# Chunked attention and a leaky two-layer MLP on one core: the order of the steps behind the first layer laid down anew, and wider filler matmuls

## The chip, the core and the metric

The kernel runs on one core of a Trainium2 chip. The core has a TensorE (PE in the profile), a VectorE (DVE), a ScalarE (ACT), a GpSimd (POOL) and a SyncE (SP), which run side by side and wait for each other by semaphores. The metric is the device time of one execution in microseconds; three runs are given and their median is compared.

## The reference

`q`, `k` and `v` have 8 batches, 8 heads, 576 rows and 64 columns. The rows are cut into chunks of 64, and each chunk attends only to itself. The result, laid out as 4608 tokens of 512 values, goes through two matrix products with a leaky ReLU between them.

```python
scores = scale * np.matmul(q_c, k_c.transpose(0, 1, 2, 4, 3))
scores = scores - np.max(scores, axis=-1, keepdims=True)
attn = np.exp(scores)
attn = attn / (np.sum(attn, axis=-1, keepdims=True) + 1e-09)
out = np.matmul(attn, v_c)
x = np.ascontiguousarray(attn_out.transpose(0, 2, 1, 3)).reshape(B * S, H * D)
h = x @ w_in                      # 4608x512 times 512x2048
g = np.maximum(0.01 * h, h)
return (g @ w_out).astype(np.float32)   # 2048x512
```

## The kernel before

**Groups.** Attention works on 36 groups of 128 tokens (two chunks), numbered u from 0. A group goes through named steps. `arrive u 0` and `arrive u 1` load q and k on the POOL queue (`load_rows`, L93). For groups 0 to 9 PE transposes them (`pe_t`, L406 and L411, into the PSUM tiles `qp` and `kp`) and ACT or DVE copies them out (`p`, L118 and L120, into QZ; `k`, L420, into KT). From group 10 on two DMA transposes on SP do it (`t u 0`, L430, into QT; `t u 1`, L433, into KT), and two POOL copies `p u 0` and `p u 1` (L446) put QT into QZ. Then come the scores `s u` on PE (L453, tile `Sp`), the maximum `m` and the subtraction `b` on DVE (L463, L467), the exponential `x` on ACT (L473), the sum and its reciprocal `z` on DVE (L479 to L483), the scaling `n` on POOL or DVE (L489, tile `en`), a transpose (`e` on PE and `d2`, or a DMA transpose `d` on SP, L508, tile `et`), the product with V `v` on PE (L519, tile `xp`) and the copy `a` on ACT into xT (L532).

**Blocks.** The MLP works on 12 blocks, four of 128 tokens and eight of 512. Blocks 0 to 5 do the first layer plainly (`mm1`, L187, tile `hT`; ACT applies the leaky ReLU, `g`, L198). Blocks 6 to 11 do it by seven half-size products (`f`, L325, tiles `hA`, `hB`, `hC`) with sums of weights (`vf`) and of inputs (`xf`, L285). Blocks 0 to 3 do the second layer plainly (`mm2`, L212, tile `oP`), blocks 4 to 11 by seven products (`m2`, L373, tiles `oA`, `oB`, `oC`) with sums `wf` and `sf`. Finished sides of a block go out by `save` on SP (L385; L391 for the last block, in six pieces).

**Order.** Nothing is decided while the kernel runs: a table `ORDER` lists every step once, with the PSUM bank or buffer that it takes, and the engines carry out their own steps in that order. A second table `ON` names the engine of those steps that could run on several. An entry such as `(86, (21, 0), 0)` puts filler matmuls ahead of step 86: 21 pieces of 128 columns into bank 0. They are made by `idle` (L538) in matmuls of up to 512 columns on constants, and their result is not used. Step 86 is `pe_t 0 1`, the first transpose on PE.

```python
def idle(n, tag):
    t = bank([128, 512], "idle", tag)
    while n:
        w = min(n, 4) * 128
        nc.tensor.matmul(out=t[:, :w], lhsT=ones[:, :128], rhs=ones[:, :w], start=True, stop=True)
        n -= w // 128
```

In the table before there are fillers ahead of `pe_t 0 1` (21 pieces), `s 0` (3), `pe_t 3 0` (47), `s 2` (13), `e 1` (9), `v 0` (9) and `v 1` (6).

Of the kernel before, what the change touches and what calls it, by code (L numbers as in the profile page):

```python
# [16 lines left out]
def kernel(  # L17
# [25 lines left out]
    NQI = 4  # L43
# [5 lines left out]
    SUB = {4: 256, 5: 256, **{j: 256 for j in range(6, 12)}}  # L49
# [3 lines left out]
    FAST = {6: 4, 7: 4, 8: 4, 9: 4, 10: 4, 11: 4}  # L53
    UNIT = {6: 256, 7: 256}
    POOL_N, POOL_X, POOL_S = 9, 20, 20
# [15 lines left out]
    qk: dict[int, tuple[bass.AP, bass.AP]] = {}  # L71

    WIN: dict[int, bass.AP] = {}

    def window(w):

        if w not in WIN:
            WIN[w] = sbp.tile([128, 2 * H * D], FP16, name="q_in", tag="q_in", bufs=NQI)
        return WIN[w]
# [4 lines left out]
    def k_tile():  # L84
        return sbp.tile([128, H, D], FP16, name="k_in", tag="k_in", bufs=NIN)
# [9 lines left out]
    def load_pairs(w):  # L95
        t = window(w).rearrange("p (h e) -> p h e", h=H)
        for a, z, b, r in cuts(2 * w * G, 2 * (w + 1) * G):
            p0, n = (a - 2 * w * G) // 2, (z - a) // 2
            nc.gpsimd.dma_start(out=t[p0:p0 + n], in_=q[b, :, r:r + z - a, :].rearrange("h (p e) d -> p h (e d)", e=2))

    def load_q(u):
        load_rows(q_tile(u), q, u)
        qk[u] = (q_tile(u), qk[u][1] if u in qk else None)

    def load_k(u):
        t = k_tile()
        load_rows(t, k, u)
        qk[u] = (qk[u][0] if u in qk else None, t)
# [49 lines left out]
    qk[0] = (q_tile(0), k_tile())  # L158
# [11 lines left out]
    def gT(j):  # L170
        n = START[j] // 512
        if n not in GT:
            GT[n] = sbp.tile([128, NFC, 512], FP16, name="gT", tag="gT", bufs=2)
        return GT[n][:, :, START[j] % 512:START[j] % 512 + BLOCKS[j]]

    def sub(j):
        return SUB.get(j, BLOCKS[j])
# [42 lines left out]
    def osb_tile():  # L220
        return sbp.tile([128, 2, d_model], FP32, name="osb", tag="osb", bufs=3)
# [58 lines left out]
    def x_form(j, h, i):  # L280
        (x11, x12), (x21, x22) = x_halves(j, h)
        f = x_sums(j, h)

        def less(to, a, b):
            (nc.gpsimd if j >= POOL_X else nc.vector).tensor_tensor(out=to, in0=a, in1=b, op=ALU.subtract)  # L285

        if i == 0:
            less(f[:, 0], x12, x11)
        elif i == 1:
            less(f[:, 1], x22, f[:, 0])  # L290
        elif i == 2:
# [47 lines left out]
    def g_form(j, i):  # L339
# [38 lines left out]
    def osb(j, side):  # L378
        if (j, side) not in OSB:
            OSB[j, side] = osb_tile()  # L380
        return OSB[j, side]
# [21 lines left out]
    def stage_tq(u, tag="qp"):  # L403
        QP[u] = psp.tile([128, 4, 2, CH], FP16, name="qp", tag=tag, bufs=1)
        for i in range(4):
            nc.tensor.transpose(out=QP[u][:, i, :, :], in_=qk[u][0][:, 2 * i:2 * i + 2, :], identity=ident)  # L406

    def stage_tk(u, tag="kp"):
        KP[u] = psp.tile([128, 4, 2, CH], FP16, name="kp", tag=tag, bufs=1)
        for i in range(4):  # L410
            nc.tensor.transpose(out=KP[u][:, i, :, :], in_=qk[u][1][:, 2 * i:2 * i + 2, :], identity=ident)  # L411
# [6 lines left out]
    def stage_k(u):  # L418
        KT[u] = sbp.tile([128, 4, 2, CH], FP16, name="KT", tag="KT", bufs=4)
# [4 lines left out]
    def stage_t(u, i):  # L424
        if i == 0:
            QT[u // 2] = sbp.tile([128, H, 128], FP16, name="QT", tag="QT", bufs=2)
            nc.sync.dma_start_transpose(out=QT[u // 2], in_=WIN.pop(u // 2))
        elif i == 2:
            QT[u] = sbp.tile([128, H // 2, 128], FP16, name="QT", tag="QT", bufs=4)
            nc.sync.dma_start_transpose(out=QT[u], in_=qk[u][0].rearrange("p h d -> p (h d)"))  # L430
        else:
            KT[u] = sbp.tile([128, 4, 2, CH], FP16, name="KT", tag="KT", bufs=4)
            nc.sync.dma_start_transpose(  # L433
                out=KT[u].rearrange("p i e t -> p i (e t)"), in_=qk[u][1].rearrange("p h d -> p (h d)")
            )
# [35 lines left out]
    def stage_x(u):  # L471
        E[u] = sbp.tile([128, 8, CH], FP16, name="ex", tag="ex", bufs=2)
# [4 lines left out]
    def stage_z(u):  # L477
        z = sbp.tile([128, 8], FP32, name="z", tag="z", bufs=2)
        nc.vector.tensor_reduce(out=z, in_=E[u], axis=AXL.X, op=ALU.add)  # L479
        ze = sbp.tile([128, 8], FP32, name="ze", tag="ze", bufs=2)  # L480
        nc.vector.tensor_scalar_add(out=ze, in0=z, scalar1=1e-9)
        ZI[u] = sbp.tile([128, 8], FP32, name="zi", tag="zi", bufs=2)
        nc.vector.reciprocal(out=ZI[u], in_=ze)  # L483

    def stage_n(u, e):
        ex = E.pop(u)
        eng = nc.gpsimd if e == "pool" else nc.vector
        E[u] = sbp.tile([128, 8, CH], FP16, name="en", tag="en", bufs=3)
# [17 lines left out]
    def stage_d(u):  # L506
        et = sbp.tile([128, 2, 2, 2, CH], FP16, name="et", tag="et", bufs=4)
# [33 lines left out]
    def cast_q():  # L541
        nc.vector.tensor_copy(out=qk[0][0], in_=first[0])

    def cast_k(h):
        half = slice(4 * h, 4 * h + 4)
        if h == 0:
            nc.vector.tensor_copy(out=qk[0][1][:, half], in_=first[1][:, half])
        else:
            nc.scalar.activation(out=qk[0][1][:, half], in_=first[1][:, half], func=AFT.Copy, bias=0.0, scale=1.0)
# [82 lines left out]
    def arrive(u, i):  # L632
        n = len(cuts(u * G, (u + 1) * G))
        old = u - (2 * NQI if i == 0 else NIN)
        after = [get(("t", old, i)) or get(("pe_t", old, i))]
        if i == 0 and u % 2 == 0:
            after.append(get(("t", old + 1, 0)) or get(("pe_t", old + 1, 0)))
        load(("arrive", u, i), 0.88, lambda: (load_q, load_k)[i](u), 980 if u < 6 else 1024, after, n=n, key=5 + u / 100)

    def arrive_v(b, c0, c1, after=(), **kw):  # L640
# [535 lines left out]
```

## Time and profile before

| | us |
|---|---|
| runs | 275.3, 275.49, 276.17; median 275.49 |
| profiled execution, span from first to last instruction | 275.7 |
| PE busy | 263.9 (96%) |
| DVE busy | 209.4 (76%) |
| ACT busy | 196.3 (71%) |
| POOL busy | 158.2 (57%) |

The profile is one execution. A busy time counts the stretches in which an engine has an instruction under way; for PE, matmuls overlap, so the spacing of their starts tells more than their durations. A wait is put down to whatever came last. A row of the timeline gives start, length, engine, line, operation, tiles and count, and in brackets how long the engine had been idle and for whom.

### The profile page before, as it was taken

Reading aid. Unit: us, or ns where it says so; the run is one execution under the profiler, and the core shown is the slowest. Engines: PE = TensorE matmul, PEld = TensorE weight load, DVE = VectorE, ACT = ScalarE, POOL = GpSimd, SP = SyncE. Lnnn points to the kernel's source line nnn. Section 1 sums busy time; section 2 is a strip of 40 time slices with the busy share of each in tenths; the row PEclk is TensorE's granted clock in tenths of the full one; section 3 lists DMA queues with packets and bytes.
Section 4 is the critical chain, followed back from the end, with each engine's and each line's share of the span. In section 5 each row is a group of like instructions: output and inputs, shape, how many; then the busy total and the mean of one; then the engine's idle time right before and its main releaser. Section 6 shows DMA issues by size and latency. Waiting matters only on the chain.

```text
span 275.7 us, 7655 instructions
## 1 busy us (share of the span) xinstructions
PE 263.9 (96%) x3099; PEld 230.8 (84%) x3099; DVE 209.4 (76%) x376; ACT 196.3 (71%) x370; POOL 158.2 (57%) x199
## 2 busy tenths in 40 slices
PE   4899999999999999999799999999999999999994
PEld 2459678788898899999799999999999989888884
DVE  5786276878889898799778997889998873825462
ACT  6478964767844834899698558899787897467821
POOL 8989685595999991928927888626752020000000
PEclk9999999999999999999999999999999999999999
DMA  9999999999999999999999999969972051040016
GB/s 133 158 190 179 179 167 175 134 157 168 172 160 148 173 173 183 132 138 223 129 131 198 138 173 199 153 148 131 212 154 40 0 137 58 0 155 0 30 49 231
DMA packets 163635, 38.64 MB, mean 140 GB/s; under 512 B 154640, under 2 KB 159248, under 8 KB 163600
## 3 DMA queue, kind: packets, MB, share of 16 engines
q0 software_dynamic: 114384, 18.09, 101.9%
q1 hardware_dynamic: 48176, 19.80, 40.1%
q8 instruction: 24, 0.39, 0.6%
q10 hardware_dynamic: 1040, 0.26, 0.4%
q14 instruction: 11, 0.09, 0.1%
HBM read 36.70 MB, written 9.44 MB: 167 GB/s over the span
## 4 chain that ended last, share of the span: by engine, by line
PE 87%; DMA 5%; ACT 5%; POOL 1%; issue 1%; POOLq 0%
PE oA L373 20%; PE hA L325 14%; PE hT L187 13%; PE oC L373 10%; PE hC L325 7%; PE oB L373 5%; PE oP L212 5%; PE hB L325 4%; PE Sp L453 3%; DMA KT<-k_in 3%; PE xp L519 3%; DMA k_in<-in_k_dram 2%; PE idle L538 1%; ACT VB L118 1%; ACT xT L532 1%; ACT gT L198 1%
## 5 line engine op out<-in xcount | busy, mean ns | idle before, releaser
L373 PEld LDWEIGHTS <-gT 128*128 128x128 f16 x640 | 61.3, 98 | 6.7
L489 POOL TENSOR_TENSOR en<-ex,zi 128x512 f16<-128x512 f16 x23 | 26.5, 1153 | 48.4 <-DVE zi L483 17.3
L237 DVE TENSOR_TENSOR tmp<-hC,tmp 128x512 f32<-128x512 f32 x48 | 32.1, 683 | 20.0 <-PE hC L325 18.3
L187 PE MATMUL hT<-xT,w_inT 128*128 128x128 f16 (+1 forms) x512 | 46.0, 246 | 1.0 <-ACT xT L532 0.9
L187 PEld LDWEIGHTS <-w_inT 128*128 128x128 f16 x512 | 39.4, 98 | 4.7 <-issue 1.3
L325 PEld LDWEIGHTS <-VF 128*128 128x128 f16 x512 | 39.4, 98 | 2.7
L93 POOL DMA_DIRECT2D q_in<-in_q_dram x39 | 33.6, 866 | 5.2 <-DMA w_outT<-in_moe_w_out_dram 2.1
L93 POOL DMA_DIRECT2D k_in<-in_k_dram x39 | 33.6, 865 | 2.3 <-DMA k_in<-in_k_dram 1.2
L446 POOL COPY QZ<-QT 64x512 f16<-64x512 f16 x52 | 33.2, 639 | 2.7 <-DMA QT<-q_in 0.5
L201 ACT ACTIVATE tmp<-hA 128x512 f32<-128x512 f32 x48 | 27.7, 598 | 8.6 <-PE hA L325 8.0
L198 ACT ACTIVATE gT<-hT 128x512 f16<-128x512 f32 x48 | 26.7, 601 | 8.6 <-PE hT L187 8.6
L373 PE MATMUL oA<-WF,gT 128*128 128x256 f16 x256 | 32.5, 273 | 0.0
L325 PEld LDWEIGHTS <-w_inT 128*128 128x128 f16 x384 | 30.2, 98 | 2.3
L463 DVE TENSOR_REDUCE mx<-Sp 128x8 f32<-128x512 f32 x36 | 24.5, 682 | 8.6 <-PE Sp L453 8.5
L198 ACT ACTIVATE gT<-tmp 128x512 f16<-128x512 f32 x48 | 29.6, 629 | 1.2 <-DVE tmp L237 1.2
L473 ACT ACTIVATE ex<-sh 128x512 f16<-128x512 f32 x36 | 22.7, 629 | 10.3 <-DVE sh L467 10.1
L479 DVE TENSOR_REDUCE z<-ex 128x8 f32<-128x512 f16 x36 | 24.3, 676 | 6.2 <-ACT ex L473 6.1
L325 PE MATMUL hA<-XF,VF 128*128 128x128 f16 (+1 forms) x256 | 27.5, 246 | 0.0
L532 ACT ACTIVATE xT<-xp 128x512 f16<-128x512 f32 x36 | 21.2, 599 | 8.7 <-PE xp L519 8.6
L373 PEld LDWEIGHTS <-S 128*128 128x128 f16 x256 | 24.5, 98 | 2.7
L467 DVE TENSOR_TENSOR sh<-Sp,mx 128x512 f32<-128x512 f32 x36 | 24.4, 683 | 0.5
L201 ACT ACTIVATE hB<-hA 128x512 f32<-128x512 f32 x24 | 13.9, 586 | 12.2 <-PE hA L325 12.1
(77 smaller groups left out, 490.3 us busy)
## 6 DMA issues: line engine op xcount, KB each, us to landing
out_dram<-osb SPq DMA_DIRECT2D x14, 512.0 KB, 4.3
VB<-in_v_dram POOLq DMA_DIRECT2D x14, 288.0 KB, 7.8
q_in<-in_q_dram POOLq DMA_DIRECT2D x31, 128.0 KB, 7.4
k_in<-in_k_dram POOLq DMA_DIRECT2D x31, 128.0 KB, 7.2
w_inT<-in_moe_w_in_dram POOLq DMA_DIRECT2D x8, 256.0 KB, 7.6
w_outT<-in_moe_w_out_dram POOLq DMA_DIRECT2D x4, 512.0 KB, 9.4
out_dram<-osb SPq DMA_DIRECT2D x6, 256.0 KB, 4.9
v_t<-in_v_dram POOLq DMA_DIRECT2D x4, 128.0 KB, 7.6
```

The lines of the kernel that those rows point to most:

```text
L93: nc.gpsimd.dma_start(out=t[a - u * G:z - u * G], in_=src[b, :, r:r + z - a, :].rearrange("h p d -> p h d"))
L187: nc.tensor.matmul(out=hT[:, i, :], lhsT=w_inT[:, t, fc * 128:(fc + 1) * 128], rhs=xT[:, t, r0 % RING:r0 % RING + tb], start=(i == 0 and t ...
L198: nc.scalar.activation(out=to, in_=of, func=AFT.Prelu, bias=0.0, scale=1.0, alpha=0.01)
L201: nc.scalar.activation(out=to, in_=of, func=AFT.Copy, bias=0.0, scale=1.0)
L237: (nc.vector if e == "dve" else nc.gpsimd).tensor_tensor(out=to, in0=a, in1=b, op=ALU.add)
L325: nc.tensor.matmul(out=PA[key][:, c, :], lhsT=w[:, t, fc * 128:(fc + 1) * 128], rhs=x[:, t, :], start=(m in (1, 5) and c == 0 and t == 0), ...
L373: nc.tensor.matmul(out=to, lhsT=lhs[:, fc, p * 128:(p + 1) * 128], rhs=rhs[:, fc, :], start=(fresh and fc == 0), stop=(fc == HB - 1), skip ...
L446: nc.gpsimd.tensor_copy(out=QZ[u % NQZ][part, :, :, s, :], in_=QT[u][part].rearrange("p i (e t) -> p i e t", e=2))
L463: nc.vector.tensor_reduce(out=MX[u], in_=SP[u], axis=AXL.X, op=ALU.max)
L467: nc.vector.tensor_tensor(out=SH[u], in0=SP.pop(u), in1=MX.pop(u).unsqueeze(2).to_broadcast((128, 8, CH)), op=ALU.subtract)
L479: nc.vector.tensor_reduce(out=z, in_=E[u], axis=AXL.X, op=ALU.add)
L489: eng.tensor_tensor(out=E[u], in0=ex, in1=ZI.pop(u).unsqueeze(2).to_broadcast((128, 8, CH)), op=ALU.mult)
```

## The change

The steps are the same, and so is what each computes. Four things differ.

- `ORDER` is another table. On every engine the first part, up to block 0's first matmuls of the first layer, has its steps in the sequence of before (the fillers aside); behind that, neighbours change places on all engines. On SP the first 22 DMA transposes and saves stay as they were, and the first to move is `t 18 0`.
- The fillers: 39 pieces ahead of `pe_t 0 1`, 9 ahead of `pe_t 1 1`, 31 ahead of `pe_t 2 1`, 79 ahead of `pe_t 3 0`, 19 ahead of `s 2`, 17 ahead of `v 0`, 4 ahead of `v 1`, 3 ahead of `mm1 0 0 0`, the first matmul of the first layer, and 2 ahead of `v 2`. In all 203 pieces where 108 stood.
- Seven steps change engine: `zv 3 2` (one of sixteen pieces of the zeros beside V) from ACT to POOL; `n 13`, `n 22` and `n 34` from POOL to DVE; `n 28` from DVE to POOL; `xf 6 0 1` and `xf 11 0 1` (one sum of inputs each) from DVE to POOL.
- Buffers that were dealt out in rotation (`bufs=4` and the like) are named by their number (`KT{u % 4}`), and q is held per group instead of per pair of groups. The number of buffers and the bytes moved are the same. Code that was switched off is gone, so line numbers shift.

```diff
@@ tables, cut @@
-        (54, 0), (53, 0), (6, 0), (86, (21, 0), 0), (83, 0, 1), (7, 0), (87, 0), (112, 0, 2), (84, 0), (115, 0, 3), (8, 0), (114, 0), (85, 0), (113, 0), (116, 0),
-        (88, (3, 4), 4), (13, 0), (144, 0, 5), (89, 0), (117, 0, 6), (145, 0), (18, 0), (90, 0), (23, 0), (118, 0), (91, 0), (119, 0), (24, 0), (92, 0), (58, 0),
...
+        (5, 0), (54, 0), (53, 0), (6, 0), (86, (39, 7), 0), (83, 0, 1), (87, 0), (112, 0, 2), (84, 0), (7, 0), (114, 0), (85, 0), (115, (9, 7), 3), (113, 0),
+        (8, 0), (88, 0, 4), (116, 0), (89, 0), (13, 0), (90, 0), (18, 0), (144, (31, 1), 5), (117, 0, 6), (145, 0), (23, 0), (118, 0), (91, 0), (119, 0),
...
@@ buffers, one of many alike @@
-            KT[u] = sbp.tile([128, 4, 2, CH], FP16, name="KT", tag="KT", bufs=4)
+            KT[u] = sbp.tile([128, 4, 2, CH], FP16, name="KT", tag=f"KT{u % 4}", bufs=1)
...
@@ q per group @@
-    def q_tile(u):
-        return window(u // 2)[:, u % 2 * H * D:(u % 2 + 1) * H * D].rearrange("p (h d) -> p h d", h=H)
+    def in_tile(what, u):
+        return sbp.tile([128, H, D], FP16, name=what, tag=f"{what}{u % NIN}", bufs=1)
...
@@ engine of the sums @@
-    def x_form(j, h, i):
+    def x_form(j, h, i, e):
...
-            (nc.gpsimd if j >= POOL_X else nc.vector).tensor_tensor(out=to, in0=a, in1=b, op=ALU.subtract)
+            minus(to, a, b, e)
```

**PE around the scores of group 4.** Before, sixteen matmuls of the first layer (`hT`) stood between the transpose of group 4's k (`kp_642`) and the scores of group 4 (`Sp_675`); the second `kp` is group 7's k. Only the matmuls are shown, one of each run; before first, then after.

```order
L406 MATMUL qp_637<-ident_84,q_in_518 128x128
...
L411 MATMUL kp_642<-ident_84,k_in_469 128x128
...
L187 MATMUL hT_647<-xT_68,w_inT_66 128x128
...
L411 MATMUL kp_670<-ident_84,k_in_545 128x128
...
L453 MATMUL Sp_675<-KT_665,QZ_65 128x64
...
```

```order
L388 MATMUL qp_665<-ident_84,q_in_537 128x128
...
L393 MATMUL kp_670<-ident_84,k_in_497 128x128
...
L393 MATMUL kp_679<-ident_84,k_in_572 128x128
...
L425 MATMUL Sp_685<-KT_677,QZ_65 128x64
...
L169 MATMUL hT_696<-xT_68,w_inT_66 128x128
...
```

The sixteen `hT` matmuls now stand behind the scores of group 4, and only the four transposes of group 7 are left between group 4's transpose and its scores.

**SP around the k of group 22.** `QT` and `KT` are the DMA transposes of q and k, `et` those of the scaled exponentials, `out_0_dram` a save. Before: `t 22 0`, `t 23 0`, `d 19`, `save 5 0`, `t 22 1`, `d 20`. After: `t 22 0`, `save 4 1`, `t 23 0`, `d 19`, `t 22 1`, `save 5 0`, `t 23 1`.

```order
L430 DMA_TRANSPOSE QT_2373<-q_in_1801 128x4x128
L430 DMA_TRANSPOSE QT_2405<-q_in_1801 128x4x128
L508 DMA_TRANSPOSE et_2443<-en_2402 128x4x128
L385 DMA out_0_dram<-osb_1952 128x2x512
L433 DMA_TRANSPOSE KT_2514<-k_in_1987 128x4x128
L508 DMA_TRANSPOSE et_2560<-en_2536 128x4x128
```

```order
L409 DMA_TRANSPOSE QT_2377<-q_in_1929 128x4x128
L367 DMA out_0_dram<-osb_1941 128x2x512
L409 DMA_TRANSPOSE QT_2423<-q_in_1835 128x4x128
L480 DMA_TRANSPOSE et_2480<-en_2447 128x4x128
L412 DMA_TRANSPOSE KT_2505<-k_in_2053 128x4x128
L367 DMA out_0_dram<-osb_2002 128x2x512
L412 DMA_TRANSPOSE KT_2553<-k_in_1675 128x4x128
```

The transpose of group 22's k has passed the save that stood ahead of it, `save 5 0`.

**POOL around the q of group 22.** `en` is a scaling `n`, `QZ<-QT` a copy `p`, the others are loads. Before: `n 19`, `p 21` twice, two loads, `n 20`, `p 22` twice. After: `p 21` twice, a load, `n 19`, `n 20`, two loads, one `p 22`, a load, the other `p 22`.

```order
L489 TENSOR_TENSOR en_2402<-ex_2336,zi_2354 128x512
L446 COPY QZ_65<-QT_1975 64x8x64 x2
L93 DMA q_in_2211<-in_q_dram 128x8x64
L93 DMA k_in_2478<-in_k_dram 128x8x64
L489 TENSOR_TENSOR en_2536<-ex_2455,zi_2484 128x512
L446 COPY QZ_65<-QT_2373 64x8x64 x2
```

```order
L418 COPY QZ_65<-QT_2000 64x8x64 x2
L79 DMA q_in_2353<-in_q_dram 128x8x64
L461 TENSOR_TENSOR en_2447<-ex_2394,zi_2416 128x512
L461 TENSOR_TENSOR en_2564<-ex_2495,zi_2531 128x512
L79 DMA k_in_2588<-in_k_dram 128x8x64
L79 DMA q_in_2617<-in_q_dram 128x8x64
L418 COPY QZ_65<-QT_2377 64x8x64
L79 DMA q_in_2647<-in_q_dram 128x8x64
L418 COPY QZ_65<-QT_2377 64x8x64
```

Three loads have come between `n 20` and the last copy of group 22's q.

More of the change, by code (lines that the diff above doesn't have):

```diff
@@ L42 @@
     BY_PE = [8, 9, 18]
-    NQI = 4
     G = 2 * CH
@@ L52 @@
     NTMP = 6
-    FAST = {6: 4, 7: 4, 8: 4, 9: 4, 10: 4, 11: 4}
-    UNIT = {6: 256, 7: 256}
-    POOL_N, POOL_X, POOL_S = 9, 20, 20
+    FAST = {j: 4 for j in range(6, 12)}
+    UNIT = {j: 256 for j in (6, 7)}
+    POOL_N = 9
     sbp = ctx.enter_context(tc.tile_pool(name="k_sb", bufs=1))
@@ L93, in load_rows @@
             nc.gpsimd.dma_start(out=t[a - u * G:z - u * G], in_=src[b, :, r:r + z - a, :].rearrange("h p d -> p h d"))
[L95 to L99, printed above, removed]
+    IN_Q: dict[int, bass.AP] = {}
+    IN_K: dict[int, bass.AP] = {}
     def load_q(u):
-        load_rows(q_tile(u), q, u)
-        qk[u] = (q_tile(u), qk[u][1] if u in qk else None)
+        IN_Q[u] = in_tile("q_in", u)
+        load_rows(IN_Q[u], q, u)
     def load_k(u):
-        t = k_tile()
-        load_rows(t, k, u)
-        qk[u] = (qk[u][0] if u in qk else None, t)
+        IN_K[u] = in_tile("k_in", u)
+        load_rows(IN_K[u], k, u)
     def load_v(b, m, c0, c1):
@@ L157 @@
     nc.vector.memset(zeros, 0.0)
-    qk[0] = (q_tile(0), k_tile())
+    IN_Q[0], IN_K[0] = in_tile("q_in", 0), in_tile("k_in", 0)
     ident = sbp.tile([128, 128], FP16, name="ident")
@@ L379, in osb @@
         if (j, side) not in OSB:
-            OSB[j, side] = osb_tile()
+            OSB[j, side] = osb_tile(2 * j - PLAIN + side)
         return OSB[j, side]
@@ L405, in stage_tq @@
         for i in range(4):
-            nc.tensor.transpose(out=QP[u][:, i, :, :], in_=qk[u][0][:, 2 * i:2 * i + 2, :], identity=ident)
+            nc.tensor.transpose(out=QP[u][:, i, :, :], in_=IN_Q[u][:, 2 * i:2 * i + 2, :], identity=ident)
     def stage_tk(u, tag="kp"):
@@ L410, in stage_tk @@
         for i in range(4):
-            nc.tensor.transpose(out=KP[u][:, i, :, :], in_=qk[u][1][:, 2 * i:2 * i + 2, :], identity=ident)
+            nc.tensor.transpose(out=KP[u][:, i, :, :], in_=IN_K[u][:, 2 * i:2 * i + 2, :], identity=ident)
     def stage_q(u, s, e):
@@ L541, in cast_q @@
     def cast_q():
-        nc.vector.tensor_copy(out=qk[0][0], in_=first[0])
+        nc.vector.tensor_copy(out=IN_Q[0], in_=first[0])
     def cast_k(h):
@@ L633, in arrive @@
         n = len(cuts(u * G, (u + 1) * G))
-        old = u - (2 * NQI if i == 0 else NIN)
+        old = u - NIN
         after = [get(("t", old, i)) or get(("pe_t", old, i))]
-        if i == 0 and u % 2 == 0:
-            after.append(get(("t", old + 1, 0)) or get(("pe_t", old + 1, 0)))
         load(("arrive", u, i), 0.88, lambda: (load_q, load_k)[i](u), 980 if u < 6 else 1024, after, n=n, key=5 + u / 100)
@@ L793, in front @@
                 load(("P", n[0]), 1.0, lambda a=n[0]: load_w_out(a), 2930)
-        for x in arrivals:
-            x.until, x.margin = 1.3, 0.2
         add(("cast", 0, 0), "dve", 0.6, cast_q, key=0, at=4.5)
@@ L811, in group @@
         by_pe = u < UD
-        pairs = 0
-        if pairs and u >= UD and u % 2 == 0 and ("arrive_q", u // 2) not in done:
-            load(("arrive_q", u // 2), 1.65, lambda: load_pairs(u // 2), 1300,
-                 [get(("t", u - 2 * NQI, 0))] + [get(("pe_t", y, 0)) for y in (u - 2 * NQI, u - 2 * NQI + 1)], n=len(cuts(u * G, (u + 2) * G)), key=5 + u / 100)
         for i in range(2):
-            if u > 0 and ("arrive", u, i) not in done and (i or by_pe or not pairs):
+            if u > 0 and ("arrive", u, i) not in done:
                 arrive(u, i)
@@ L974, in first_fast @@
         inf = [get(("vf", q)) for q in range(4)]
-        p1 = mm(1, 0, xs + gone(j) + [get(("fast", x)) for x in fast_n[-LIMIT:-LIMIT + 1]], [A], spare=SPARE + 1)
+        w11 = [get(("Q", q, m)) for q in range(2) for m in range(2)]
+        p1 = mm(1, 0, xs + gone(j) + w11 + [get(("fast", x)) for x in fast_n[-LIMIT:-LIMIT + 1]], [A], spare=SPARE + 1)
         d = add(key + ("d",), "act", 0.5, seed, [p1], key=6.9 + k0 / 100, take=[B1])
@@ L1070, in second_fast @@
             c21.append(add(key + ("c21", p), "act", us[0], lambda p=p: copy(dest(1, lo, p), psum("oA", p)), ([p4[p]] if last else p4) + saves[-2:-1], key=7.2 + k0 / 100, give=[A[p]]))
-        s12 = sum_of("u2", 0, hi, two(p3, u2), B2)
+        s12 = sum_of("u2", 0, hi, [x + osb_free() for x in two(p3, u2)], B2)
         if last:
```

125 lines of the change are left out of this document (52 added, 73 removed), and 227 rows, old and new, of tables (ON, ORDER).

## The prediction

> **What bounds the kernel now.** I read the page first, then the stretches of the span, then PE's idle rows and, at each, the engine that was waited for. The page gives shares per engine, and the chain of waits:
>
> ```profile
> span 275.7 us, 7655 instructions
> PE 263.9 (96%) x3099; PEld 230.8 (84%) x3099; DVE 209.4 (76%) x376; ACT 196.3 (71%) x370; POOL 158.2 (57%) x199
> PE 87%; DMA 5%; ACT 5%; POOL 1%; issue 1%; POOLq 0%
> ```
>
> PE is the bound. What an order can still give is PE's idle time. The stretches (start and end in us, PE's busy time, matmuls, granted clock, DMA) say where it lies:
>
> ```profile
> 20.00:74.00 54.00, 53.62 (x688) 1.00 1.99 167
> 74.00:76.00 2.00, 1.31 (x19) 1.00 2.17 144
> 76.00:132.00 56.00, 55.78 (x756) 1.00 1.91 165
> 132.00:135.00 3.00, 1.29 (x30) 1.00 1.21 106
> 135.00:272.00 137.00, 137.00 (x1516) 1.00 1.02 117
> 272.00:276.00 4.00, 0.22 (x2) 1.00 0.38 135
> ```
>
> From 20 us on PE is idle for 0.38 + 0.69 + 0.22 + 1.71 = 3.0 us, and after 135 not at all until its end. Then come 3.7 us of the last copy and save, whose PE steps stand in the same order in both tables. So behind the front only 3 us are to be had, and the front of 20 us is the other place. The idle rows of PE's timeline (in brackets the idle time before, and for whom):
>
> ```profile
> 30.02 0.40 PE L497 MATMUL tpe<-ident,en 128*128 128x128 f16 x4 [0.26 <-ACT gT L198]
> 75.71 1.47 PE L187 MATMUL hT<-xT,w_inT 128*128 128x256 f16 x12 [0.69 <-ACT xT L532]
> 131.94 0.61 PE L325 MATMUL hC<-XF,VF 128*128 128x128 f16 x8
> 132.39 0.61 PE L325 MATMUL hA<-XF,VF 128*128 128x128 f16 x8
> 134.71 0.39 PE L453 MATMUL Sp<-KT,QZ 128*128 128x64 f16 x8 [1.71 <-DMA KT<-k_in]
> ```
>
> The product at 132.39 is issued in 0.45 us, like the one ahead of it, so PE came to the scores of group 22 at 132.84 and began them at 134.71: 1.87 us lost. In the new table the first-layer matmul at 75.71 still stands right behind the `v 9` whose copy it needs, and `e 3` at 30.02 behind the same work of ACT; those waits stay, at no change.
>
> **The k of group 22.** SP's timeline and the chain's piece for this transpose:
>
> ```profile
> 122.52 1.43 SPq L430 DMA_TRANSPOSE QT<-q_in  x1
> 124.47 1.20 SPq L508 DMA_TRANSPOSE et<-en  x1
> 126.61 0.38 SPq L385 DMA_DIRECT2D out_dram<-osb  x1
> 127.16 1.96 SPq L433 DMA_TRANSPOSE KT<-k_in  x1
> ...
> 127.16 7.41 DMA KT<-k_in
> ```
>
> `t 22 1` stood behind `save 5 0`, which SP held until 126.61. With the save behind it, it goes at 124.47 + 1.20 + 0.1 = 125.8, and lands 7.41 later at 133.2. PE comes there at 132.84, plus one product moved ahead (0.45) and the 0.64 found below: 133.9. So the k no longer stops PE. Next late is the q:
>
> ```profile
> 126.40 0.88 POOL L93 DMA_DIRECT2D k_in<-in_k_dram  x1
> 127.85 1.04 POOL L489 TENSOR_TENSOR en<-ex,zi 128x512 f16<-128x512 f16 x1 [0.57 <-ACT gT L198]
> 128.95 1.41 POOL L446 COPY QZ<-QT 64x512 f16<-64x512 f16 x2
> 130.31 1.82 POOL L93 DMA_DIRECT2D q_in<-in_q_dram  x2
> ```
>
> Now three loads stand between `n 20` and the last `p 22`. From the end of `n 20`: 0.88 + 0.91 + 0.70 + 0.91 + 0.70 = 4.1 us. `n 20` itself moves, because `v 16`, `e 18` and one product went ahead of `s 20` on PE (0.24 + 0.22 + 0.45 = 0.9, and the 0.64: 1.55 later). DVE's queue is full there and hides part of it; the ends are 0 and 1.55, and I take 1.0, since DVE is also rid of `d2 18` ahead of it. `n 20` ends at 128.9 + 1.0, the last `p 22` at 134.0, PE starts at 134.1: a wait of 0.2, with ends 0 and 0.75. Term: -1.87 + 0.2 = **-1.67**.
>
> **The scores of group 4.** PE's and ACT's rows:
>
> ```profile
> 35.25 0.39 PE L411 MATMUL kp<-ident,k_in 128*128 128x128 f16 x4
> 35.47 1.06 PE L187 MATMUL hT<-xT,w_inT 128*128 128x128 f16 x16
> 36.36 0.39 PE L411 MATMUL kp<-ident,k_in 128*128 128x128 f16 x4
> 36.59 0.40 PE L453 MATMUL Sp<-KT,QZ 128*128 128x64 f16 x8
> ...
> 35.67 0.60 ACT L420 ACTIVATE KT<-kp 128x512 f16<-128x512 f16 x1 [0.35 <-PE kp L411]
> ```
>
> ACT was waiting for this transpose, and its copy ends at 36.27. Before, the `hT` matmuls covered that; now PE is through with group 7's transposes at 35.47 + 0.22 = 35.69 and waits for `KT` until about 36.33. Nothing behind it on PE can pass. Ends: 0.3 (if ACT's copies shift) and 0.9. Term: **+0.64**, at work that nothing gives back, as PE is busy from there on.
>
> **The fillers.** PE's timeline up to 18 us, and the chain of waits:
>
> ```profile
> 1.46 2.42 PE L538 MATMUL idle<-XF 128*128 128x512 f16 x6 [1.46 <-DVE zeros L157]
> 5.94 0.58 PE L411 MATMUL kp<-ident,k_in 128*128 128x128 f16 x4 [2.06 <-POOL ident masks.py:199]
> 7.60 0.53 PE L538 MATMUL idle<-XF 128*128 128x384 f16 x1
> 8.28 0.59 PE L453 MATMUL Sp<-KT,QZ 128*128 128x64 f16 x8
> 9.92 0.61 PE L411 MATMUL kp<-ident,k_in 128*128 128x128 f16 x4 [1.05 <-DMA k_in<-in_k_dram]
> 15.64 0.87 PE L538 MATMUL idle<-XF 128*128 128x512 f16 x4
> 17.11 0.65 PE L538 MATMUL idle<-XF 128*128 128x512 f16 x3
> ...
> 10.95 3.99 PE idle L538 x12
> 14.98 0.62 PE qp L406 x8
> ```
>
> A piece has two prices. 13 pieces took 0.87 and 9 took 0.65: 0.055 us each. Earlier 21 took 2.42 and 3 took 0.53: 0.105 each. The 47 pieces of 3.99 us are then 28 slow and 19 fast ones, so PE's clock doubled near 13.9. (The page's row of the granted clock reads 9 throughout, so only the spacing tells.)
>
> 39 pieces at 0.105 end at 1.46 + 4.1 = 5.6, inside the wait for `ident` that ended at 5.94: free. From there it hangs on the clock. Fast by then: `s 0` at 8.28 as before, 31 pieces from 8.5 to 10.2, the transposes and `s 1` at 0.22 and 0.24 to 10.7, 79 pieces at 0.055 to 15.0, where 14.98 stood. The other fillers fill PE's waits before `s 2` and `v 0`; the last 5 pieces (0.3 us) go into the wait at 30.02. Slow until 13.9: 9 pieces put `s 0` at 8.55, 31 pieces end at 12.3, `s 1` at 13.1, the 79 near 17.8: 2.8 later, all on the chain of waits, since `qp` starts it anew. Between the two (clock up at 10.3), 1.1 later. On the gain side, `s 0` could come 0.3 earlier. I take **0**, with ends -0.3 and +2.8, because in the trace 3 to 4 us of PE's work from 9.92 brought the fast clock, and 39 pieces are 4.1 us.
>
> [...]
>
> **Other moves.** Seven steps change engine: DVE gets three scalings and gives one and two sums; each is at most 1.1 us (the POOL row above) beside 66 us of DVE idle: 0 on the path. ACT is rid of 0.7 us of zeros: 0, since no PE row waits for it. Further on PE comes to the scores of group 25 by 3.2 us of moved work and to those of group 26 by 4.3 us earlier than before. The rows of group 25:
>
> ```profile
> 148.50 1.04 POOL L489 TENSOR_TENSOR en<-ex,zi 128x512 f16<-128x512 f16 x1 [1.82 <-DVE zi L483]
> 151.78 1.32 POOL L446 COPY QZ<-QT 64x512 f16<-64x512 f16 x2
> 159.26 0.40 PE L453 MATMUL Sp<-KT,QZ 128*128 128x64 f16 x8
> ```
>
> Its q was ready 6.2 us early. Now PE is earlier by 3.2 + 1.0 and its last copy is queued behind `p 26` twice and a load, some 2.2 later: near 0 left. I put **+0.3** for such places together, with ends 0 and 1.5.
>
> **Sum.** 0 + 0.64 - 1.67 + 0.3 = -0.73, so 274.9 for the profiled execution (275.67) and 274.8 against the median of the runs (275.49, 0.2 below it). That is -0.27%; about 0.3% (0.83 us) is what a measurement of this kernel can tell from no change, so it lies just inside.
>
> **Rivals.**
> - *Everything behind the front fits* (no wait at `s 22`, none later, `s 0` earlier): 0.64 - 1.87 - 0.3 = -1.5, or -1.9 if ACT's copy comes sooner: 273.6 to 274.0. For it: after 135 the trace has not one idle row on PE. Against: the places above have under 1 us left. Chance 0.25.
> - *The clock is still slow when the 31 and 79 pieces run*: the front is 1.1 to 2.8 later, 275.9 to 277.6, slower where it is more than 1.6. It decides at about 9 us, when the 31 pieces start. For it: only 9.92 to 13.9 is shown to bring the clock, and a wait of 0.3 us and transposes follow the 39 pieces. Against: 4.1 us of work. Chance 0.15.
> - *New waits take the place of the old*: POOL's order costs 0.75 at `s 22`, and groups 25 and 26 another 1 to 1.5: 275.5 to 276.5. For it: SP and POOL carry out their queues in order, and one save cost 1.87. Chance 0.2.
> - The forecast, 274.2 to 275.5: 0.4.
>
> Of these, faster takes the first and a third of the forecast; slower takes the greater part of the second and a quarter of the third. The forecast's own range is 274.2 to 275.5; with the rivals, 273.5 to 276.9.
>
> **What would show it.** `Sp` of group 22 with under 0.8 us of idle before it, named for `QZ` if any; a new idle row of PE near 36, for ACT `KT`; filler pieces at 0.055 from about 6 us; PE at `qp` near 15.0. Wrong: slow pieces past 9 us, or idle rows of over 0.5 us after 135.

## The result: slower by 1.2%, and the profile after

The changed kernel took 279.96 us in the median of 17 runs (277.69 to 283.76), the kernel before 275.95 in as many (275.05 to 278.92). The ratio of after to before is 1.0122, with a 95% interval of 1.0096 to 1.0149; it leaves out the changed kernel's three longest runs (281.92 and more), which count as slow, and so lies below the quotient of the two medians. The forecast was 274.8 and its range ended at 276.9: wrong in sign and outside the range.

The page of the changed kernel, with the lines that answer to those of before (span; busy time of each engine; shares of the chain of waits):

```profile
span 277.2 us, 7703 instructions
PE 267.6 (97%) x3122; PEld 231.5 (84%) x3122; DVE 211.3 (76%) x376; ACT 194.0 (70%) x369; POOL 160.8 (58%) x200
PE 85%; ACT 5%; DMA 3%; POOL 3%; DVE 1%; issue 1%; SPq 0%; POOLq 0%; DVEq 0%
```

PE is still the bound. Its 23 additional instructions are fillers, and POOL has come into the chain with 3%. The stretches behind the front (start and end, length, busy time and count of PE, of its weight loads, of DVE, ACT and POOL, then the granted clock of PE as a share of full speed, DMA share and GB/s):

```profile
20.00:74.00 54.00, 53.35 (x675) 43.40 (x673) 36.50 (x69) 39.36 (x74) 42.04 (x51) 1.00 2.02 170
132.00:153.00 21.00, 20.97 (x316) 19.89 (x314) 19.10 (x34) 18.06 (x35) 15.05 (x19) 1.00 1.87 154
153.00:158.00 5.00, 3.26 (x42) 2.73 (x41) 4.93 (x8) 1.22 (x4) 4.82 (x6) 1.00 2.10 105
182.00:185.00 3.00, 2.51 (x30) 2.06 (x28) 1.95 (x5) 2.69 (x6) 2.30 (x3) 1.00 1.90 164
185.00:272.00 87.00, 87.00 (x876) 78.26 (x874) 60.55 (x97) 61.61 (x120) 17.76 (x20) 1.00 0.57 90
```

The hole that stood before 135 us is gone, and 1.74 us are missing between 153 and 158, where before PE was never idle. PE's rows there and at the other places of which the prediction spoke (in brackets the idle time before a row, and for whom; where the text says what PE lost, it counts from where PE would have gone on at its usual spacing, which is about 0.16 us more than the bracket):

```profile
35.70 0.39 PE L425 MATMUL Sp<-KT,QZ 128*128 128x64 f16 x8 [0.46 <-ACT KT L402]
75.71 3.65 PE L169 MATMUL hT<-xT,w_inT 128*128 128x256 f16 x32 [0.68 <-ACT xT L504]
133.38 0.40 PE L425 MATMUL Sp<-KT,QZ 128*128 128x64 f16 x8
156.26 0.41 PE L425 MATMUL Sp<-KT,QZ 128*128 128x64 f16 x8 [1.74 <-POOL QZ L418]
183.75 0.39 PE L491 MATMUL xp<-et,VB 128*128 128x64 f16 x8 [0.49 <-DVE zi L455]
```

The scores of group 22 (133.38) wait for nothing, which lies within the ends of the forecast (0 to 0.75), and those of group 4 (35.70) wait for ACT's `KT`, as forecast. New are the scores of group 25 at 156.26 and the product with V of group 27 at 183.75. The chain of waits shows what group 25 waited for, with POOL's and DVE's rows of the last copy behind it:

```profile
143.80 8.62 DMA QT<-q_in
...
152.57 0.54 POOL QZ L418
...
153.12 0.88 POOL q_in L79
...
154.05 0.61 POOL QZ L418
...
154.69 1.52 POOL QZ L418
...
156.26 0.41 PE Sp L425 x8
...
152.57 0.61 POOL L418 COPY QZ<-QT 64x512 f16<-64x512 f16 x1 [1.33 <-DMA QT<-q_in]
...
154.05 2.16 POOL L418 COPY QZ<-QT 64x512 f16<-64x512 f16 x2
154.15 1.58 DVE L219 TENSOR_TENSOR S<-gT 128x2048 f16<-128x2048 f16 x1
```

On POOL the new table has `p 25 0`, a load, `p 26 1`, a load, `p 26 0`, `p 25 1`. `p 26 1` had to wait 1.33 us for group 26's DMA transpose (143.80, landed at 152.42), and `p 25 1`, which needs nothing of group 26, stood behind it. Its copy then took 1.52 us where the one ahead of it took 0.61; over the whole trace the copies of this line took 0.60 to 1.67, with a median of 0.61. A DVE sum of two inputs (154.15 to 155.73) was under way beside both, so whether it lengthened the second is not shown. The wait and the longer copy together, 1.33 + 0.91 = 2.2 us, are more than the 1.9 that PE lost there.

**The base of the sum.** Every run lists its span beside its time, and the time is 1.7 to 1.95 us more: 279.03 and 277.2 for this profile, 275.6 and 273.8 for a run of the kernel before. The profile of before, of span 275.7, was therefore an execution of about 277.5, and not one near the median of 275.49. Of the 95 executions of the kernel before that were timed beside the experiments, two had a span of 275.7 or more; most lie between 273.5 and 274.5. One of these ordinary executions is seen in the fifth experiment.

### The profile page after: what moved, and what is told of

It reads as the page before. It is cut to its first block, busy times and chain, and to the rows that moved or that the text cites. A ratio compares the mean times of both kernels' runs of the same rounds, so it can differ in the third digit from the quotient of the medians.

```text
span 277.2 us, 7703 instructions
## 1 busy us (share of the span) xinstructions
PE 267.6 (97%) x3122; PEld 231.5 (84%) x3122; DVE 211.3 (76%) x376; ACT 194.0 (70%) x369; POOL 160.8 (58%) x200
## 4 chain that ended last, share of the span: by engine, by line
PE 85%; ACT 5%; DMA 3%; POOL 3%; DVE 1%; issue 1%; SPq 0%; POOLq 0%; DVEq 0%
PE oA L355 19%; PE hA L307 15%; PE hT L169 13%; PE oC L355 9%; PE hC L307 7%; PE oP L194 5%; PE oB L355 4%; PE hB L307 4%; DMA QT<-q_in 3%; PE Sp L425 3%; PE xp L491 3%; PE idle L510 2%; ACT VB L100 1%; ACT xT L504 1%; POOL QZ L418 1%
## 5 line engine op out<-in xcount | busy, mean ns | idle before, releaser
L461 POOL TENSOR_TENSOR en<-ex,zi 128x512 f16<-128x512 f16 x21 | 24.2, 1154 | 33.3 <-DVE zi L455 14.9
L418 POOL COPY QZ<-QT 64x512 f16<-64x512 f16 x52 | 36.4, 703 | 11.7 <-DMA QT<-q_in 8.2
L183 ACT ACTIVATE tmp<-oA 128x512 f32<-128x512 f32 (+1 forms) x27 | 14.9, 551 | 9.8 <-PE oA L355 9.7
```

What stands on the lines that cost most here:

```text
L183: nc.scalar.activation(out=to, in_=of, func=AFT.Copy, bias=0.0, scale=1.0)
L418: nc.gpsimd.tensor_copy(out=QZ[u % NQZ][part, :, :, s, :], in_=QT[u][part].rearrange("p i (e t) -> p i e t", e=2))
```

## Experiments

Each was timed beside the kernel before on the same chip (its median was 275.6 to 275.9 on the five chips used), the two single executions excepted; each ratio is to the kernel before on that chip. Intervals are 95% of the ratio to it.

### The two halves of the change

The changed kernel again:

> The changed kernel once more, beside the kernel before on the same chip, for its spans and a second trace. Both theories: 278 to 281 us against 275 to 277.

Measured: 280.2 us (279.2 to 281.94), ratio 1.0166 [1.0141, 1.0192]. In its trace PE lost 0.63 us before group 4's scores, 1.68 before group 25's, and now 0.69 near 192 and 0.46 near 200, but not the 0.66 near 183: some of the waits change from execution to execution.

The old order with the new fillers:

```diff
-(86, (21, 0), 0)  (88, (3, 4), 4)  (170, (47, 7), 7)  (146, (13, 2), 2)
+(86, (39, 0), 0)  (115, (9, 3), 3)  (144, (31, 5), 5)  (170, (79, 7), 7)  (146, (19, 2), 2)
...
```

> The order of before with the wider fillers. Theory 1 (the order behind the front is what costs, by waits for DMA transposes at places with under 1 us to spare): 275 to 276, the same as before or up to 0.6 us faster, since the changed kernel's profile has its first layer start at 19.33 us and not at 19.98. Theory 2 (the wider fillers cost, since they hold the front up in executions where TensorE's clock comes late): 278 to 280.

Measured: 277.87 us (276.57 to 279.03), ratio 1.0078 [1.0054, 1.0101], between the two ranges. The fillers alone cost 2 us. In its trace block 0's first layer begins at 20.03, and the scores of group 23 wait for their k, a wait that the trace of the ordinary execution below does not have:

```profile
144.77 0.39 PE L453 MATMUL Sp<-KT,QZ 128*128 128x64 f16 x8 [1.98 <-DMA KT<-k_in]
```

So what is seen of the cost there is in part the front and in part a transfer behind it.

The new order with the old fillers:

```diff
-(86, (39, 7), 0)  (115, (9, 7), 3)  (144, (31, 1), 5)  (170, (79, 4), 7)  (146, (19, 6), 2)
+(86, (21, 0), 0)  (88, (3, 4), 4)  (170, (47, 7), 7)  (146, (13, 2), 2)
...
```

> The new order with the fillers of before. Theory 1: 278.5 to 280.5, as the changed kernel or a little above it. Theory 2: 275 to 276.5.

Measured: 280.51 us (277.23 to 281.75), ratio 1.0137 [1.0091, 1.0182], although its front came 0.85 us earlier than that of the changed kernel (block 0's first layer at 18.48 and 19.33). The order alone costs as much as the whole change, so the costs of the two halves do not add up.

The changed kernel without the wait of group 25:

```diff
 POOL: ... p 25 0
+      p 25 1
       arrive 28 1, p 26 1, arrive 29 0, p 26 0
-      p 25 1
```

> The changed kernel with one step moved: the second POOL copy of group 25's q stands right behind the first, ahead of group 26's copies and two loads. Theory 1: the 1.9 us wait ahead of the scores of group 25 goes, and 1 to 2 us of the time with it. Theory 2: that wait goes, but the time stays within 0.5 us of the changed kernel.

Measured: 280.08 us (276.6 to 281.87), ratio 1.0164 [1.012, 1.0208]. In the profiled execution the wait was gone and the span was 274.8, 2.4 less than before the edit. The median did not move, but the six executions fall into two sets: three took 276.6 to 278.9, and three 281.2 to 281.9. What the move is worth is therefore unclear, and the largest visible wait was not the whole loss. This trace does not show the reason of the three long ones; their mean granted clock, 0.990 to 0.994 against 0.997 to 1.000 in the other three, points to a stretch at a lower clock. A trace of such an execution follows under "The long executions".

### Which part of the order

Tables can be mixed, since the steps are numbered alike: the first 446 steps (to about 91 us) are the same set in both, and the first 930 (to about 172 us) but for one. Banks are renamed at a cut. First the new code with the old table throughout:

```diff
-ORDER = NEW
+ORDER = OLD
```

> The new code (buffers named by number, q held per group) with the order, fillers and engines of before throughout. Theory A (the loss is in the order of single places): the code does nothing, 275.4 to 276.0 us as before, runs within 1.3 us of each other. Theory B (any shift against the DMA transfers costs, since before's order was fitted to its own timing): same, because nothing shifts; if the buffers themselves cost, 277 or more.

Measured: 276.02 us, ratio 1.0005 [0.9982, 1.0028]. The rewritten buffers cost nothing (its executions lie 3.2 us apart, not 1.3). Its trace is the ordinary execution of the old order (span 273.5). Its front, PE's rows and the chain's piece of group 3's q, and then group 22:

```profile
9.06 0.40 PE L425 MATMUL Sp<-KT,QZ 128*128 128x64 f16 x8
9.29 2.70 PE L510 MATMUL idle<-XF 128*128 128x512 f16 x12
13.66 0.62 PE L388 MATMUL qp<-ident,q_in 128*128 128x128 f16 x8 [1.66 <-DMA q_in<-in_q_dram]
...
6.75 6.86 DMA q_in<-in_q_dram
...
132.47 0.39 PE L425 MATMUL Sp<-KT,QZ 128*128 128x64 f16 x8 [0.78 <-DMA KT<-k_in]
```

Beside the profile of before: group 1's k is there early, so its scores begin at 9.06 and not at 10.32; the 47 pieces ahead of `qp` are all fast (2.70 us); `qp` begins at 13.66, when group 3's q has landed, and not at 14.98; and group 22 costs 0.95 us, not 1.87 (its scores begin at 132.47, and PE was through with the product of 131.08 at 131.08 + 0.44 = 131.52). These account for the 2.2 us between the two spans.

Then each third of the new order within the old one, with the old fillers:

```diff
-ORDER = OLD
+ORDER = NEW[:446] then OLD
```

> The new order up to the 446th step (about 91 us), the old order, fillers and engines of before behind it. Theory A: the stretch holds only the wait of the scores of group 4 (+0.6), and the front with before's fillers came 1.5 us earlier in the run with the new order, so 274.3 to 276.5. Theory B: what stands behind 91 us meets its transfers 1 us off, so 277.5 to 280 with a scatter of 3 us.

Measured: 277.13 us, ratio 1.0047 [1.0027, 1.0066]. This lies between the ranges of the two theories. In its trace the wait of group 4 is 0.63, and group 22 waits 1.29 instead of 0.95.

```diff
-ORDER = OLD
+ORDER = OLD[:446] then NEW up to 930, then OLD
```

> The old order with the new one only from the 446th to the 930th step (about 91 to 172 us). Theory A: the stretch holds the wait of the scores of group 25 (1.7 to 1.9 us), so 277.3 to 278.5, and the wait shows in the trace before the scores of group 25. Theory B: the shift begins only at 91 us, so the scatter is that of half the span, 276.5 to 279.

Measured: 278.25 us, ratio 1.0083 [1.0047, 1.0118]. PE's and POOL's rows at group 25:

```profile
157.00 0.41 PE L425 MATMUL Sp<-KT,QZ 128*128 128x64 f16 x8 [2.44 <-POOL QZ L418]
154.37 2.57 POOL L418 COPY QZ<-QT 64x512 f16<-64x512 f16 x2
```

The wait of group 25 lies in this third alone, as expected, and was larger than the range that the expectation gave it.

```diff
-ORDER = OLD
+ORDER = OLD[:930] then NEW
```

> The old order with the new one only behind the 930th step (about 172 us). Theory A: the stretch holds the small wait of PE near 183 us (0.3 to 0.7) and a tail 0.6 us longer, so 276.2 to 277. Theory B: a small part of the loss, 276 to 277.5. If the three thirds add up to the 4.9 us of the whole new order with before's fillers, the loss is made of single places; if each third alone is near 0 or each alone costs 3 or more, it is not.

Measured: 277.22 us, ratio 1.0034 [1.0013, 1.0055]. PE lost 0.36 near 173 and 0.37 near 197, and the time from PE's last matmul to the end was 4.2 us instead of 3.8. The three thirds add up to 0.47 + 0.83 + 0.34 = 1.64%, the whole order gave 1.37%, within its interval. The loss is spread over all three; the middle has the most by its median figure, though its interval overlaps with that of the first.

### The fillers

```diff
-(170, (79, 7), 7)
+(170, (47, 7), 7)
```

in the kernel with the old order and the new fillers:

> The order of before with the new fillers, but 47 pieces instead of 79 ahead of the first transpose of group 3. In the trace of the old order in the new code (273.5 us span) the load of group 3's q landed at 13.61 and its transposes began at 13.66; with the new fillers the 8 and 20 filler matmuls from 7.96 on kept PE until 14.4 to 14.8. Theory A (the fillers overrun a load that lands earlier in most executions than in the profile of before): 32 pieces fewer are 1.7 us, so the transposes begin within 0.1 us of the load again, block 0's first layer at 18.6 to 19.0 and the median falls from 277.9 to 275.8 to 276.6. Rival (the fillers cost by their power or by the clock, or by the later wait at 142 us): 277.3 to 278.2, as with 79.

Measured: 275.5 us (274.24 to 277.46), ratio 0.9988 [0.9967, 1.001]: 2.4 us less than with 79, and a little under the range of theory A. With 79 (the changed kernel) and with 47 (this one), PE's rows:

```profile
7.96 1.84 PE L510 MATMUL idle<-XF 128*128 128x512 f16 x8
10.10 4.43 PE L510 MATMUL idle<-XF 128*128 128x512 f16 x20
14.36 0.61 PE L388 MATMUL qp<-ident,q_in 128*128 128x128 f16 x8
...
10.40 2.70 PE L538 MATMUL idle<-XF 128*128 128x512 f16 x12
13.16 0.61 PE L406 MATMUL qp<-ident,q_in 128*128 128x128 f16 x8
```

Twenty matmuls hold PE until 14.36, although the q that `qp` needs had landed by 12.96 and at 13.61 in the two traces in which PE waited for it (the kernel with 47 that follows, and the ordinary execution); twelve are through at 13.1. The front is not the whole of the 2.4 us, though: over all traces block 0's first layer begins between 18.45 and 20.09 with 47 pieces there (12 traces, median 18.9; in some of them a k load that is issued near 10.3 lands late), and between 19.17 and 20.03 with 79 (8 traces, median 19.6). That is 0.7 us, so the rest must have come behind the front. The wait of group 23 above is such a place, and this trace has none there; whether it comes in every execution no run shows. The same edit within the changed kernel:

```diff
-(170, (79, 4), 7)
+(170, (47, 4), 7)
```

> The changed kernel with 47 fillers instead of 79 ahead of the first transpose of group 3, nothing else. Theory A: the first layer of block 0 begins at 18.6 to 18.9 instead of 19.3 to 19.6, so 0.6 to 0.9 less: 279.1 to 279.4 in the median, with the scatter of the new order as it was. Rival: the time gained in the front is given back at the next transfer (280).

Measured: 279.41 us (279.16 to 281.82), ratio 1.0143 [1.011, 1.0175]. The first layer began at 18.50, so the front gave 0.8 us, but in the profiled execution PE lost 2.41 us before the product with V of group 27, for its `et`. The median lies at the end of the theory's range, and the ratio lies between the two of the changed kernel (1.0122 and 1.0166), so theory and rival cannot be told apart here: in the new order no gain from fewer fillers shows clear of the scatter.

### A version faster than both

The one wait that the change was right about, taken alone: on SP, in the old order,

```diff
-t 22 0, t 23 0, d 19, save 5 0, t 22 1, d 20
+t 22 0, t 22 1, d 19, t 23 0, save 5 0, d 20
```

> The old order, fillers and engines in the new code; on SP alone the transpose of group 22's k goes right behind that of its q, and that of group 23's q behind the transpose for group 19. Theory: PE waited 0.86 to 1.87 us for that k in five traces of the old order; the k now lands 3 us earlier, the wait goes, 274.9 to 275.2. Rival (the next late thing, group 19's or group 23's transposes, takes its place): 275.6 to 277.5.

Measured: 275.16 us (274.0 to 276.05) against 275.82, ratio 0.997 [0.9951, 0.9988]. SP's and PE's rows:

```profile
122.54 1.48 SPq L412 DMA_TRANSPOSE KT<-k_in  x1
132.01 0.61 PE L307 MATMUL hA<-XF,VF 128*128 128x128 f16 x8
132.45 0.40 PE L425 MATMUL Sp<-KT,QZ 128*128 128x64 f16 x8
```

The wait of group 22 is gone, and in the trace no other of over 0.2 us has come behind it; it is the only kernel of this study whose interval lies below 1.

### The long executions

Single executions with their traces, first of the changed kernel, then of it with `p 25 1` moved:

> The changed kernel once more, one execution with its trace. [...]

> The changed kernel with the last copy of group 25's q moved up on POOL, one execution with its trace. Of six executions three took 281.2 to 281.9 at a granted clock of 0.990 to 0.994 and the other three 276.6 to 278.9. [...]

Both were long ones, 280.95 and 281.14 us. In the first, DVE's and PE's rows:

```profile
21.56 2.21 DVE L453 TENSOR_SCALAR ze<-z 128x8 f32<-128x8 f32 x1
24.79 0.40 PE L469 MATMUL tpe<-ident,en 128*128 128x128 f16 x4 [1.90 <-DVE en L461]
```

A DVE instruction on 8 columns took 2.21 us (0.37 in the profile of the result) while POOL ran a load and its memsets, and the chain through `n 2` made PE lose 2.06; another 0.96 went near 95 and 1.08 near 185. Group 25 cost only 0.33 there. In the second, the chain's piece, PE's row, and the stretches around it:

```profile
136.48 11.88 DMA et<-en
148.50 0.59 PE L491 MATMUL xp<-et,VB 128*128 128x64 f16 x8 [3.07 <-DMA et<-en]
145.00:148.50 3.50, 0.43 (x9) 0.28 (x6) 1.18 (x4) 0.25 (x1) 0.00 (x0) 0.95 2.06 104
148.50:150.00 1.50, 1.50 (x19) 1.50 (x20) 0.00 (x0) 0.88 (x2) 1.48 (x2) 0.50 1.77 156
150.00:152.00 2.00, 2.00 (x17) 1.69 (x15) 1.17 (x2) 1.70 (x4) 1.94 (x4) 0.62 1.66 156
152.00:154.00 2.00, 2.00 (x34) 1.91 (x33) 1.34 (x2) 0.32 (x1) 2.00 (x4) 1.00 1.87 157
```

The DMA transpose for group 20 landed 11.88 us after its issue; those of the same kind between 118 and 150 us had a median of 7.3. In the new table it is issued at 136.48, 7.3 us later than in the old one (129.22 in the profile of before), and PE was through with the product ahead of it at 145.3, so PE waited 3.07 us. Then the granted clock was 0.50 and 0.62 in the next two rows: 0.75 + 0.76 = 1.5 us more. In the trace of the middle third, with its wait of 2.44, the mean granted clock was 1.000. The late transfer and the slow stretch behind it come to 4.6 us; that the wait brought the clock down is my reading of this one trace. In the first, waits alone made a long execution: its mean granted clock is 1.000, and of its three large losses only the one near 185, at the product with V of group 27, stands where the profile of the result had lost time as well. The second has a long wait elsewhere and the lower clock behind it. The large waits of the two share no place. A lower mean clock is not rare: 16 of the 155 executions of the changed kernel and its variants have a mean granted clock of 0.994 or less, and all 16 took 280.0 us or more; this second trace has 0.991, every other profiled execution 0.997 or more.

### Queues or compute engines

Both tables give each engine a sequence, and the sequences can be merged crosswise: PE, ACT and DVE from one table, POOL and SP from the other.

```diff
-PE, ACT, DVE: OLD    POOL, SP: OLD
+PE, ACT, DVE: NEW    POOL, SP: OLD
```

> PE, ACT and DVE run in the new order, POOL and SP (the queues that load, transpose and save) in the old one, with the fillers of before; the new order throughout with these fillers took 280.5 (+4.9). Theory D (the loss comes from the queues: transposes and copies issued later than before): the loss is gone but for the scores of group 4 (0.6) and the small waits near 183: 275.8 to 277. Rival E (the loss comes from PE arriving earlier or in another order at transfers that are no later): 278 to 281.

```diff
-PE, ACT, DVE: OLD    POOL, SP: OLD
+PE, ACT, DVE: OLD    POOL, SP: NEW
```

The seven steps that change engine go with this second kernel; the first has them on their old engines.

> The reverse: PE, ACT and DVE in the old order, POOL and SP in the new one, fillers of before. Theory D: the transpose for group 20 still goes 8 us later on SP and the copies of group 25's q later on POOL, so waits at the product with V of group 20 and the scores of group 25: 278 to 281 with a scatter of 4 us. Rival E: 275 to 276.5.

Measured: 279.43 us, ratio 1.0133 [1.0093, 1.0174], for the new compute order; 276.73 us, ratio 1.0032 [1.001, 1.0054], for the new queues. I had expected the reverse: theory D fell. The second lies a little above the range of its rival. In the first, PE waits for transposes that have kept their places on SP:

```profile
134.62 0.39 PE L425 MATMUL Sp<-KT,QZ 128*128 128x64 f16 x8 [1.37 <-DMA KT<-k_in]
142.95 0.39 PE L425 MATMUL Sp<-KT,QZ 128*128 128x64 f16 x8 [1.72 <-DMA KT<-k_in]
```

The second row is group 23, whose scores the new table puts ahead of 2.2 us of PE's work; those of groups 25, 26 and 30 it puts ahead of 3.3, 4.4 and 3.3. Neither of the two traces has the wait of group 25: it was seen only where both halves are new, so the two ratios do not say where the waits of the changed kernel belong.

### Repairs

Two thin places of the queues in the changed kernel, `p 25 1` as above and on SP:

```diff
 save 5 0, t 23 1
+d 20
 t 24 1, t 24 0, t 25 0, save 5 1
-d 20
```

> The changed kernel with two steps of the queues put earlier: the last copy of group 25's q on POOL, and the DMA transpose for group 20 on SP ahead of the transposes for groups 24 and 25 and a save (it is issued near 131 instead of 136). In the traces of the new order it landed 6 to 12 us after its issue, and PE's product with V for group 20 stood at 145.2. Theory: the waits of 0.2 to 3.2 us there, and the window of PE's half clock behind the longest, go with the wait of group 25: 276.8 to 278, and the executions of 281 and more are gone. Rival: the executions of 281 come from other places as well (DVE's 2.2 us instruction in the front, 1.1 us near 184): 279 to 280, with some at 281.

Measured: 278.67 us (277.96 to 279.83), ratio 1.0102 [1.0073, 1.013]. This lies between the ranges of theory and rival. No execution reached 280, where 12 of the 23 of the changed kernel in its two series did, and the mean granted clock was 0.997 or more in all six. The same holds for the last kernel below, the other one with `d 20` put earlier; of the 49 executions of the whole new order with `d 20` at its late place, 11 had 0.994 or less. That fits the late transpose as one cause of the clock's drop; it is not the only one, as three of the six executions of the new compute order, with `d 20` at its old place, had 0.994 too. But PE now lost 1.52 us before the product with V of group 27 (`182.70`, for `et`). Then PE's own steps:

```diff
 PE
-s 25 behind m2 7 2 1; s 26 behind m2 6 4 1
+s 25 behind v 23; s 26 behind m2 7 5 0
-v 26 behind v 25; v 27 behind m2 8 1 0; mm1 3 0 0 behind s 4
+v 26 behind m2 7 4 1; v 27 behind m2 7 3 1; mm1 3 0 0 behind pe_t 4 1
```

> The changed kernel with five steps of PE put back to the neighbours they had before, and nothing on POOL or SP: the scores of groups 25 and 26 behind 3.3 and 3.5 us more of PE's work, the products with V of groups 26 and 27 behind one and two more matmul groups, and one first-layer step again between the last transpose and the scores of group 4. Theory E (PE reaches these steps before their data): the waits of 0.6 (group 4), 1.7 to 1.9 (group 25) and 0.5 to 2.4 (group 27) go, 276.6 to 278.0. Rival: others take their place, 279 to 281.

Measured: 281.52 us (278.79 to 283.69), ratio 1.0169 [1.0118, 1.022]. This is above the ranges of both. The waits of groups 4 and 25 were gone, and the time was not less. Its trace, and below it that of the next kernel:

```profile
183.72 0.39 PE L491 MATMUL xp<-et,VB 128*128 128x64 f16 x8 [1.14 <-DMA et<-en]
188.32 1.03 PE L307 MATMUL hA<-XF,VF 128*128 128x256 f16 x8 [0.72 <-ACT hB L183]
...
176.06 0.41 PE L425 MATMUL Sp<-KT,QZ 128*128 128x64 f16 x8 [0.61 <-POOL QZ L418]
187.17 1.03 PE L307 MATMUL hA<-XF,VF 128*128 128x256 f16 x8 [0.72 <-ACT hB L183]
```

The row of `hB` is of my own making: `v 27` moved back on PE, but ACT's sequence stayed, in which the copy of `v 27` stands ahead of the one that the product at 188.32 needs, and ACT waited 1.85 us for it. All repairs together:

> The same five steps put back, and the three repairs tried before together: 47 fillers instead of 79, the last copy of group 25's q earlier on POOL, the transpose for group 20 earlier on SP. Theory: these places are the loss: 0.7 less from the front and no executions above 279, so 275.2 to 276.6, within 0.3% of before. Rival: half of the loss lies spread over the rest of the order: 277.5 or more.

Measured: 278.58 us (277.07 to 280.65), ratio 1.0101 [1.0047, 1.0156]. The rival holds: the named places, put back, recover perhaps a third of the loss, and less than that is not excluded.

## Why the prediction was wrong

**The base.** The sum was made against 275.67 as if it were an execution near the median. It was 2 us above. Of the two things that made it so, the late loads of the front (1.3) and a long wait of group 22 (1.87 instead of 0.95), the prediction took the one for the front's normal state and the other for a gain to be had in every execution. The term -1.67 had the right mechanism and place; taken alone the repair is worth 0.7 us (275.82 to 275.16).

**The fillers, taken at 0.** The clock did double early, as forecast: pieces at 0.054 from 6.8 us on, where the 39 ahead of them had taken 4.34 (0.11 each), and with a wait of 0.18 and transposes in between; so the rival of a slow clock did not come about. But the place that the 31 and 79 pieces were to fill was that of the unusual execution, in which PE reached its own 47 pieces only at 10.76. Where PE waited for the q, it had landed by 12.96 and at 13.61, and the 79 pieces held PE until 14.36 and, in the old order, 14.84. In the old order the fillers cost 2 us with the 79 and nothing with 47 (-0.1%); some 0.7 of it is the front, and the rest is put behind it, where one trace shows a wait of 1.98 (group 23). The upper end of +2.8 covered it, by another mechanism. In the new order their part does not show: 1.0137 with the old fillers, 1.0143 with 47, 1.0122 and 1.0166 with 79.

**The scores of group 4, +0.64.** Right: 0.62 in the profile of the result and 0.4 to 0.63 in the other traces with that order, for ACT's `KT`.

**Thin places, +0.3.** This is the step that failed most. The prediction had found PE 3.2 us earlier at group 25 and its last copy 2.2 later, "near 0 left", and took 0.3 for all such places, with an upper end of 1.5. The order alone cost 1.37%, or 3.8 us; with group 4 at +0.6 and group 22 at -0.7, as measured, the rest of the order cost some 3.9 where the sum had 0.3. In the six traces with both new orders there, group 25 alone lost 0.1 to 2.6, in four of them 1.7 and more. It had counted the copies at their usual 0.6 to 0.7 (one took 1.52), and had not followed the copies of group 26, behind which `p 25 1` stands, back to their transpose (a wait of 1.33). And it had asked whether a step is late in one execution; the DMA transposes of the traces land from 2.4 to 11.9 us after their issue. That a place with under 2 us left therefore pays in some executions and not in others fits the scatter at group 25; it was not tried by itself.

**The rivals.** "New waits take the place of the old" is what happened, with a chance of 0.2 and 275.5 to 276.5. Its mechanism, POOL's and SP's queues, is worth 1 us by itself (ratio 1.0032); the order of PE, ACT and DVE by itself costs more (1.0133), and the prediction saw that only at groups 4, 25 and 26.

**What stays open.** Which steps of the compute engines' order hold the loss. It is in all three thirds, it is not in the five PE steps alone that were put back, and the places of the waits differ from execution to execution. That the new order has less time between a transfer's issue and its use in many places, each of which strikes now and then, fits all runs, but it was not shown by a run that gives the time back and recovers the whole. The tail, 4.3 us instead of 3.8 from PE's last matmul to the end, was seen in each kernel with the whole new last third and was not tried by itself; the sum had put the end at no change.

## What to carry to other kernels

Before a sum is made against a profile, hold its span against those of ordinary runs: a profile is one execution, and a wait or a covered gap in it may be that execution's alone. Fillers are sized for the earliest arrival of what they wait for, not for the latest. And an order is as good as its margins: for each transfer, compare the time from its issue to its use with the spread of its landing times, because bringing PE earlier to a place gains nothing once the data set the pace.

## What the runs showed of the hardware

- A wait of 3.07 us on PE was followed by 1.5 us at a granted clock of 0.50 and 2 us at 0.62, which cost another 1.5; behind waits of 2.25 and 2.44 in two other traces PE went on at its usual spacing, and their mean clocks were 0.997 and 1.000.
- The landing of a DMA transpose varied: 6.40 and 7.41 for the same one of group 22 in two executions of the old order, 11.88 for one of group 20.
- Of two POOL copies of one form, both beside the same two-input sum on DVE, the first took 0.61 us and the second 1.52; a DVE instruction on 8 columns took 2.21 in one execution and 0.37 in another, both times beside POOL's loads.
- The first loads of the program landed at other times from one execution to another (the k of group 1 at 9.87, and early enough for scores at 9.06; the q of group 3 by 12.96 and at 13.61), and block 0's first layer moves with them (18.67 and 19.98 with one order and the same fillers).
